# GpSimd's subtractions and scalings in pieces of 128 columns and of two token tiles

## The chip, the core and the metric

The kernel runs on one core of a Trainium2 chip. The core has five engines that work in parallel and each run their instructions in the order given: TensorE (PE, matrix products; its weight loads are shown as PEld), VectorE (DVE), ScalarE (ACT), GpSimd (POOL) and SyncE (SP, which here only issues DMAs). They wait for each other through semaphores. The metric is the time of one execution on the device, in microseconds (us); lower is better.

## The reference

Four batches of 10048 tokens with 128 channels go through agent attention (49 agents) and then through a mixture of 16 experts in 4 groups:

```
a2k = softmax(scale * agents @ k.T);  agent_v = a2k @ v
q2a = softmax(scale * q @ agents.T);  x = q2a @ agent_v
g = argmax(x @ w_group);  e = argmax(x @ w_expert[g])        # one expert per token
out = g_w * e_w * (relu(x @ w1[g, e]) @ w2[g, e])            # g_w, e_w: softmax weights
```

All inputs and the output are float32.

## The kernel before

A batch is cut into 79 token tiles of 128 tokens, and the loads into chunks of 8 tiles (1024 columns of the transposed k or q). Float32 values are split into two float16 numbers, a high and a low part, so that TensorE can multiply them at float16 speed. For a chunk of k or q: SP loads `xf`; ACT copies it to float16 (`xh`); POOL subtracts, `xl = xf - xh` (function `low`, in pieces of `PIECE` columns); TensorE then computes the scores of the 8 tiles against the agents, three products a tile (`xh` with the agents' high and low part, `xl` with the high part). The product with `xl` waits for the piece of `xl` that holds its tile.

For queries, DVE subtracts the maximum, ACT takes the exponential (`ef`) and copies it to float16 into `rows`, POOL subtracts again (the low part, columns NA to 2 NA of `rows`; `query_split`), TensorE transposes `rows` (`et`), and computes the router's logits from it. For keys, DVE takes running maxima (`mch`), ACT the exponential, and TensorE the agent values.

Routing, the counts of tokens per expert and the choice of the batch's most frequent expert are long chains of small DVE operations (`routing`, `output_weight`, `peaks` with its tile `pm`, `signed_weights` with the tiles whose names begin with f, p and m, `cntf` and `hot`). They end in weights for the batch (`wbuf`).

The main stream (`first`, `second`, `check`) multiplies each group of four tiles with those weights: products `ph`, ACT and DVE make `hh` and `hl` from them, products `po`, and the check `pv`. `rows_out` brings the result into SBUF: for batches after the first ACT copies it (`oo`) and POOL multiplies it by the token's weight `cw`, two tiles at a time; otherwise DVE does both at once. SP stores it.

The order of the work on every engine is fixed by the string `PLAN`: each letter takes the next step of one stream (m the main stream, a agents, q queries, w routing and weights, s stores, g gathers), and all engines are pinned to that order. Before it, `front` lays out the first batch by the list `ORDER`. Both stay as they are.

Of the kernel before, what the change touches and what calls it, by code (L numbers as in the profile page):

```python
# [22 lines left out]
P = 128  # L23
B = 4
N = 10048
C = 128
# [69 lines left out]
FEW = 3 * CT  # L96
ETS = 28
LAG = 3
PIECE = 2 * P
BUSY = [3, 12]  # L100


# [93 lines left out]
def build(ctx, tc, qT, kT, v, agT, wr, w1, w2, cpk, out):  # L196
    nc = tc.nc
    pe, vec, act, pool, sync = [Pinned(x) for x in (nc.tensor, nc.vector, nc.scalar, nc.gpsimd, nc.sync)]
# [83 lines left out]
    state = {}  # L282
# [30 lines left out]
    def split_steps(kind, b, ci):  # L313
# [10 lines left out]
        yield FINE  # L324
        low(pool, PIECE, xf, xh, xl, n // 2)
        yield FINE
        low(pool, PIECE, xf, xh, xl, n, n // 2)
        return xh, xl

    def low(eng, step, xf, xh, xl, n, first=0):  # L330
        for i in range(first, n, step):
            y = slice(i, min(i + step, n))
            eng.tensor_sub(out=xl[:, y], in0=xf[:, y], in1=xh[:, y])
# [145 lines left out]
    def front(b, early, order, later):  # L479
# [34 lines left out]
        for x in order:  # L514
# [16 lines left out]
            elif o in "lL":  # L531
                xf, m = hold[c]
                xh, xl = hold["x", f"h{c}" if o == "l" else "q"]
                if o == "l" and c in POOLED:
                    low(pool, PIECE, xf, xh, xl, m)
                else:
# [57 lines left out]
            elif o == "G":  # L594
                vec.tensor_copy(out=se, in_=small[0:NA, P + NA:P + NA + 1])
            elif o == "r":
                all_of(query_split(b, 0, query, True))
            elif o == "t":
                all_of(query_turn(b, 0, query, True))
# [89 lines left out]
    def queries_of(b, early=None, cs=None, *more):  # L689

        cs = list(range(len(chunks))) if cs is None else cs
        xs = [{} for _ in chunks]
        stages = [query_load, query_scores, query_exp, query_split, query_turn]
        groups = [[lambda b, ci, x, early: load_only("q", b, ci)]] + [stages[:1], stages[1:2], stages[2:4], stages[4:]]

        def run(group):
            def f(i):
                for stage in group:
                    yield from stage(b, cs[i], xs[cs[i]], early)
            return f  # L700

        yield from skewed(len(cs), *[run(g) for g in groups], *[lambda i, f=f: f(b, cs[i]) for f in more])
# [26 lines left out]
    def query_split(b, ci, x, early):  # L729
        t0, t1 = chunks[ci]  # L730
        ef = x["ef"][:, 0:t1 - t0]
        if early and ci % 2 == 0:
            pool.tensor_copy(out=rows[:, t0:t1, 0:NA], in_=ef)
        else:
            act.activation(rows[:, t0:t1, 0:NA], ef, AF.Copy)
        yield FINE
        whole = early or b == 0 and ci <= FIRST
        for i in range(0, t1 - t0, t1 - t0 if whole else 3):
            y = slice(i, t1 - t0 if whole else min(i + 3, t1 - t0))
            w = slice(t0 + y.start, t0 + y.stop)  # L740
            (vec if whole else pool).tensor_sub(out=rows[:, w, NA:2 * NA], in0=ef[:, y], in1=rows[:, w, 0:NA])
        yield
# [579 lines left out]
    def natural(b, w):  # L1322

        t, n = TILES[w]
        return dict(b=b, w=w, t=t, n=n, per=1, units=FULL, et=state[b]["et", w], apart=b > 0 and (b < LB or w < NW - 2),
                    wb=wbuf[b % 2].bitcast(F16), done=rows_out, **signed(w, 1, MODES))
# [4 lines left out]
    def rows_out(x):  # L1331

        po, b, n, t = x["po"], x["b"], x["n"], x["t"]
        o = mo.tile([P, TQ, C], F32, name="oo", bufs=4)
        if x["apart"]:
            act.activation(o[:, 0:n], po[:, 0:n], AF.Copy)
            yield
            for i in range(0, n, 2):
                y = slice(i, min(i + 2, n))
                pool.tensor_mul(out=o[:, y], in0=o[:, y], in1=state[b]["cw"][:, t + y.start:t + y.stop].broadcast_to([P, y.stop - y.start, C]))  # L1340
                if y.stop == n:
                    written.append((b, n, t, o))
                yield
        else:
            vec.tensor_mul(out=o[:, 0:n], in0=po[:, 0:n], in1=state[b]["cw"][:, t:t + n].broadcast_to([P, n, C]))
            written.append((b, n, t, o))
            yield
# [510 lines left out]
```

## Time and profile before

| | |
|---|---|
| median of 3 runs | 803.74 us (799.58 to 804.38) |
| the profiled execution | 802.54 us, span 800.7 us |
| busy share of the span | PE 84%, DVE 80%, ACT 63%, POOL 47% |
| POOL: subtractions for xl | 284 operations, 196 us |
| POOL: scalings of oo | 116 operations, 73.8 us |
| POOL: subtractions for rows | 108 operations, 43.6 us |

The span runs from the first to the last instruction in the trace. A row of the profile groups operations of one engine with the tiles that they write and read; "128x256 f16<-128x256 f32" is 128 partitions by 256 columns, output and input. Nearly all operations have the line of one helper (L180), so they are told apart by their tiles. The granted clock of TensorE is given as a share of 2.4 GHz; a stretch with a value between 0.5 and 1 mixes both levels. In the chain of waits, each piece is the work that the next one had to wait for. The number after x is the count of operations that a row merges.

### The profile page before, as it was taken

The numbers are of one execution on the slowest core, as the hardware profiler recorded it, in microseconds if no ns is written. First come the engines' busy times: TensorE is split into PE (matmuls) and PEld (weight loads), VectorE is DVE, ScalarE is ACT, GpSimd is POOL, SyncE is SP. The second block draws the span as 40 slices with busy tenths as digits, with TensorE's granted clock in tenths as the row PEclk, the third lists the DMA queues.
The fourth block names the chain that finished last, engine by engine and source line by source line (L and its number), as shares of the span: only waits on it lengthen the run. The fifth ranks groups of instructions, "written<-read, shape, count | busy, mean of one in ns | idle before, by whom it ended". The sixth has DMA issues, their size and how long they took to land.

```text
span 800.7 us, 22170 instructions
## 1 busy us (share of the span) xinstructions
PE 671.0 (84%) x8835; PEld 535.4 (67%) x8835; DVE 641.5 (80%) x1449; ACT 501.1 (63%) x1087; POOL 378.7 (47%) x619
## 2 busy tenths in 40 slices
PE   7864879989956799999766847789999989999994
PEld 6653758767844587788545736676788667877773
DVE  6869978967789785777998897968978998866663
ACT  4544479779934446899455323545968787467772
POOL 4126393139922433587365316852565233842220
PEclk9975889999977699999878965999999999999997
DMA  8845043695607518352285032155422444211211
GB/s 320 326 159 169 28 148 106 181 359 150 193 18 258 182 31 292 96 156 79 83 299 171 1 105 69 30 152 170 123 72 83 126 174 125 71 52 54 68 54 54
DMA packets 66273, 107.87 MB, mean 135 GB/s; under 512 B 5223, under 2 KB 46136, under 8 KB 65776
## 3 DMA queue, kind: packets, MB, share of 16 engines
q1 hardware_dynamic: 64816, 104.54, 40.3%
q0 software_dynamic: 1344, 1.82, 1.0%
q8 instruction: 71, 1.16, 0.6%
q14 instruction: 42, 0.34, 0.1%
HBM read 73.97 MB, written 32.47 MB: 133 GB/s over the span
## 4 chain that ended last, share of the span: by engine, by line
PE 43%; DVE 23%; issue 6%; ACT 4%; DMA 4%; POOL 4%; SPq 0%; POOLq 0%; ACTq 0%; DVEq 0%
PE at L180 16%; PE po L180 15%; PE ph L180 8%; PE pv L180 4%; DVE hl L180 2%; DVE pm L180 2%; DVE hot L180 2%; POOL xl L180 2%; DMA vf<-v 1%; DMA out<-oo 1%; POOL oo L180 1%; DMA xf<-qT 1%; DVE rd L180 1%; DVE oh L180 1%; DVE mch L180 1%
## 5 line engine op out<-in xcount | busy, mean ns | idle before, releaser
L180 POOL TENSOR_TENSOR xl<-xf,xh 128x256 f16<-128x256 f32 (+2 forms) x280 | 193.4, 722 | 158.7 <-ACT xh L180 149.2
L180 DVE SCALAR_TENSOR_TENSOR hl<-ph,hh 128x512 f16<-128x512 f32 (+1 forms) x256 | 172.2, 678 | 77.4 <-ACT hh L180 76.2
L180 PE MATMUL po<-wbuf,hh 128*128 128x128 f16 x1896 | 194.4, 225 | 0.0
L180 PEld LDWEIGHTS <-hh 128*128 128x128 f16 x2022 | 166.3, 101 | 34.4 <-issue 4.7
L180 PE MATMUL po<-wbuf,hl 128*128 128x128 f16 x948 | 178.8, 225 | 2.6 <-DVE hl L180 2.6
L180 ACT ACTIVATE hh<-ph 128x512 f16<-128x512 f32 (+1 forms) x256 | 152.0, 594 | 32.5 <-PE ph L180 28.0
L180 PE MATMUL ph<-et,wbuf 98*128 98x512 f16 x480 | 148.8, 393 | 5.2 <-ACT spare L180 4.6
L180 ACT ACTIVATE spare<-pv 128x512 bf16<-128x512 f32 (+1 forms) x164 | 97.4, 594 | 80.3 <-PE pv L180 70.0
L180 POOL TENSOR_TENSOR oo<-oo,cw 128x256 f32<-128x256 f32 x116 | 73.8, 656 | 130.8 <-ACT oo L180 120.4
L180 PEld LDWEIGHTS <-hl 128*128 128x128 f16 x1011 | 101.7, 101 | 3.1 <-DVE hl L180 3.1
L180 PE MATMUL pv<-et,wbuf 98*128 98x512 f16 x240 | 95.1, 396 | 0.1
L180 ACT ACTIVATE xh<-xf 128x1024 f16<-128x1024 f32 (+2 forms) x78 | 81.2, 1045 | 12.5 <-DMA xf<-kT 7.8
L180 PEld LDWEIGHTS <-wbuf 98*128 98x128 f16 x720 | 61.4, 102 | 35.6 <-issue 13.8
L180 PEld LDWEIGHTS <-et 98*128 98x128 f16 x1264 | 66.2, 100 | 22.6 <-issue 4.9
L180 PE MATMUL at<-agh,xl 128*128 128x49 f16 (+1 forms) x545 | 60.9, 192 | 19.1 <-POOL xl L180 18.9
L180 PEld LDWEIGHTS <-xh 128*128 128x128 f16 (+1 forms) x1264 | 64.8, 101 | 17.2 <-ACT xh L180 7.1
L180 PEld LDWEIGHTS <-xl 128*128 128x128 f16 (+1 forms) x632 | 54.3, 99 | 25.9 <-POOL xl L180 24.3
L180 POOL TENSOR_TENSOR rows<-ef,rows 128x147 f16<-128x147 f32 (+1 forms) x108 | 43.6, 432 | 57.7 <-ACT rows L180 46.0
L180 PE MATMUL at<-agh,xh 128*128 128x49 f16 (+1 forms) x545 | 61.6, 191 | 6.7 <-ACT xh L180 6.1
L180 DVE TENSOR_REDUCE flags<-pv 128x1 f32<-128x512 f32 (+1 forms) x92 | 62.2, 677 | 5.0 <-PE pv L180 4.9
L180 PE MATMUL at<-agl,xh 128*128 128x49 f16 (+1 forms) x545 | 61.1, 191 | 0.0
L180 PE MATMUL at<-vf,S 128*49 128x129 f32 (+1 forms) x632 | 45.5, 282 | 8.8 <-ACT S L180 5.8
(369 smaller groups left out, 1275.4 us busy)
## 6 DMA issues: line engine op xcount, KB each, us to landing
xf<-qT SPq DMA_DIRECT2D x38, 512.0 KB, 5.3
out<-oo SPq DMA_DIRECT2D x76, 256.0 KB, 4.0
vf<-v SPq DMA_DIRECT2D x36, 516.0 KB, 5.1
xf<-kT SPq DMA_DIRECT2D x35, 512.0 KB, 4.8
erow<-rows SPq DMA_DIRECT2D x3, 1975.0 KB, 7.5
wsl<-wkept SPq DMA_DIRECT2D x6, 544.0 KB, 4.2
w2f<-w SPq DMA_DIRECT2D x6, 512.0 KB, 4.5
w1f<-w SPq DMA_DIRECT2D x5, 512.0 KB, 4.9
```

The source lines that it names most:

```text
L180: y = f(*a, **k)
```

## The change

`PIECE` goes from 256 to 128 columns, so a chunk of 1024 columns is subtracted in eight operations and not in four. In `query_split` the pieces of `rows` hold two tiles and not three: a chunk of eight tiles has four pieces (2, 2, 2, 2) and had three (3, 3, 2). In `rows_out` each tile of `oo` is scaled by an operation of its own; the steps of the generator are the same two tiles, so `PLAN` meets the same number of steps.

```diff
-PIECE = 2 * P
+PIECE = P
...
         whole = early or b == 0 and ci <= FIRST
-        for i in range(0, t1 - t0, t1 - t0 if whole else 3):
-            y = slice(i, t1 - t0 if whole else min(i + 3, t1 - t0))
+        for i in range(0, t1 - t0, t1 - t0 if whole else 2):
+            y = slice(i, t1 - t0 if whole else min(i + 2, t1 - t0))
             w = slice(t0 + y.start, t0 + y.stop)
             (vec if whole else pool).tensor_sub(out=rows[:, w, NA:2 * NA], in0=ef[:, y], in1=rows[:, w, 0:NA])
...
             for i in range(0, n, 2):
-                y = slice(i, min(i + 2, n))
-                pool.tensor_mul(out=o[:, y], in0=o[:, y], in1=state[b]["cw"][:, t + y.start:t + y.stop].broadcast_to([P, y.stop - y.start, C]))
-                if y.stop == n:
+                for y in range(i, min(i + 2, n)):
+                    pool.tensor_mul(out=o[:, y], in0=o[:, y], in1=state[b]["cw"][:, t + y].broadcast_to([P, C]))
+                if y + 1 == n:
                     written.append((b, n, t, o))
```

POOL's order late in the second batch's queries (about 200 to 217 us of the trace), before; `xl` is the low part of a chunk, `rows` the float16 pair of the queries' exponentials, the last column the shape and the count:

```order
L180 TENSOR_TENSOR xl<-xf,xh 128x256 x6
L180 TENSOR_TENSOR rows<-ef,rows 128x3x49 x2
L180 TENSOR_TENSOR rows<-ef,rows 128x2x49
L180 TENSOR_TENSOR xl<-xf,xh 128x256 x3
L180 TENSOR_TENSOR xl<-xf,xh 128x192
L180 TENSOR_TENSOR xl<-xf,xh 128x256
L180 TENSOR_TENSOR xl<-xf,xh 128x192
```

The same place after the change:

```order
L180 TENSOR_TENSOR xl<-xf,xh 128x128 x12
L180 TENSOR_TENSOR rows<-ef,rows 128x2x49 x4
L180 TENSOR_TENSOR xl<-xf,xh 128x128 x7
L180 TENSOR_TENSOR xl<-xf,xh 128x64
L180 TENSOR_TENSOR xl<-xf,xh 128x128 x3
L180 TENSOR_TENSOR xl<-xf,xh 128x64
```

Nothing has moved: each operation stands where its larger one stood, in two parts. The half chunk of 448 columns becomes three pieces of 128 and one of 64.

TensorE at the scores of a chunk, where the product with `xl` waits for POOL (the rest of TensorE's order is the same):

```order
 L180 LDWEIGHTS xh
 L180 MATMUL ph<-agl,xh 128x49
-L180 LDWEIGHTS xl
+L180 LDWEIGHTS xl [waits Pool_49]
 L180 MATMUL ph<-agh,xl 128x49
 L180 LDWEIGHTS xh
```

The second tile of each pair now has a wait of its own, where it had stood behind that of the first. DVE, ACT and SP have the same instructions in the same order.

## Rows read from the trace of the kernel before

**Rows 1.** The page's part 1: busy time, share, instructions.

```profile
PE 671.0 (84%) x8835; PEld 535.4 (67%) x8835; DVE 641.5 (80%) x1449; ACT 501.1 (63%) x1087; POOL 378.7 (47%) x619
```

**Rows 2.** Stages: length, busy us of PE, PEld, DVE, ACT, POOL, then clock, DMA.

```profile
60.00:118.00 58.00, 39.22 (x503) 32.74 (x502) 52.20 (x129) 32.86 (x63) 38.26 (x61) 0.72 0.38 119
170.00:218.00 48.00, 44.69 (x831) 36.30 (x832) 36.09 (x73) 44.27 (x89) 44.51 (x82) 1.00 0.69 211
340.00:382.00 42.00, 42.00 (x716) 34.19 (x714) 32.02 (x54) 39.22 (x81) 34.34 (x64) 1.00 0.40 115
382.00:425.00 43.00, 30.57 (x328) 21.94 (x326) 38.85 (x72) 23.18 (x51) 22.67 (x27) 0.80 0.53 180
```

**Rows 3.** Chain of waits, 168 to 218 us: start, us, what.

```profile
197.20 2.56 POOL xl L180 x4
199.79 0.94 POOL rows L180 x3
200.93 2.57 POOL xl L180 x4
```

**Rows 4.** POOL's instructions in time: start, us, what; the second merges two shapes.

```profile
183.36 5.08 POOL L180 TENSOR_TENSOR xl<-xf,xh 128x256 f16<-128x256 f32 x8
...
367.30 2.33 POOL L180 TENSOR_TENSOR xl<-xf,xh 128x256 f16<-128x256 f32 x4
```

**Rows 5.** POOL's groups by shape: busy us, mean ns, idle us before and its releasers.

```profile
L180 POOL TENSOR_TENSOR xl<-xf,xh 128x256 f16<-128x256 f32 x266 | 186.3, 731 | 158.7 <-ACT xh L180 149.2 <-PE at L180 9.3
L180 POOL TENSOR_TENSOR oo<-oo,cw 128x256 f32<-128x256 f32 x114 | 73.0, 661 | 130.8 <-ACT oo L180 120.4 <-issue 10.4
L180 POOL TENSOR_TENSOR rows<-ef,rows 128x147 f16<-128x147 f32 x72 | 32.4, 471 | 57.7 <-ACT rows L180 46.0 <-PE ph L180 10.0 <-PE at L180 1.6
L180 POOL TENSOR_TENSOR rows<-ef,rows 128x98 f16<-128x98 f32 x32 | 11.6, 363 | 0.0
...
L180 POOL TENSOR_TENSOR oo<-oo,cw 128x128 f32<-128x128 f32 x2 | 0.8, 395 | 0.0
```

**Rows 6.** POOL alone by stage, for xl, then rows, then oo.

```profile
170.00:218.00 48.00, 34.05 (x54) 1.00 0.69 211
...
340.00:382.00 42.00, 17.73 (x28) 1.00 0.40 115
...
170.00:218.00 48.00, 10.68 (x27) 1.00 0.69 211
...
340.00:382.00 42.00, 7.60 (x20) 1.00 0.40 115
...
340.00:382.00 42.00, 9.55 (x16) 1.00 0.40 115
```

**Rows 7.** DVE in time: two operations beside POOL's xl, two without POOL.

```profile
66.52 0.59 DVE L180 SCALAR_TENSOR_TENSOR fva<-fqq,fmu 128x8 f32<-128x8 f32 x1
67.14 0.60 DVE L180 TENSOR_SCALAR fva<-fva 128x8 f32<-128x8 f32 x1
...
279.39 0.17 DVE L180 TENSOR_TENSOR pinc<-ways 128x16 f32<-128x16 f32 x1
279.60 0.17 DVE L180 TENSOR_TENSOR pinc<-pinc,pun 128x16 f32<-128x16 f32 x1
```

**Rows 8.** DVE in time: hot without POOL, and beside it.

```profile
280.21 0.88 DVE L180 TENSOR_SCALAR hot<-wide,ppos 128x512 f16<-128x512 f16 x3
...
439.45 4.49 DVE L180 TENSOR_SCALAR hot<-wide,ppos 128x512 f16<-128x512 f16 x8
```

**Rows 9.** Waits of PE: whole span, 60 to 118 us, 382 to 425 us: us, times, longest.

```profile
PE at L180 <- POOL xl L180: 18.9, 43, 1.2
...
PE at L180 <- DVE cntf L180: 6.3, 1, 6.3
...
PE at L180 <- POOL xl L180: 9.3, 14, 1.2
```

**Rows 10.** POOL in time, from 405.4 us: eight pieces beside DVE's pm.

```profile
406.12 9.70 POOL L180 TENSOR_TENSOR xl<-xf,xh 128x256 f16<-128x256 f32 x8 [2.28 <-ACT xh L180]
```

## The prediction

> **What bounds the kernel now.** I read the page's busy shares first. TensorE (PE) is busy for 84% of the span, VectorE (DVE) for 80%, ScalarE (ACT) for 63% and GpSimd (POOL) for 47% [rows 1], so no engine is the bound throughout, and an average says nothing about POOL. The table by stage says it: from 170 to 218 us POOL is busy for 44.51 of 48.00 us, beside ACT at 44.27 and PE at 44.69; from 340 to 382 us POOL has 34.34 of 42.00 and PE is full; from 60 to 118 and from 382 to 425 us DVE is the fullest (52.20 of 58.00, 38.85 of 43.00), POOL has room, and the granted TensorE clock is 0.72 and 0.80 of full speed, a mix of the two levels 1.2 and 2.4 GHz [rows 2]. So two kinds of stage have to be kept apart: in the first POOL paces, in the second DVE's chain of small operations paces and POOL only disturbs it. The chain of waits confirms the first: from 197.2 to 203.5 us it runs through POOL alone, four subtractions of xl, three of rows, four of xl [rows 3].
>
> **The change, part by part.** The order is unchanged on every engine; operations are split in place. DMAs and queues are the same. TensorE waits for xl once per 128 columns in place of once per 256, and I cost those waits at nothing, since they only matter where the piece is late.
>
> *Price of a split.* Four xl pieces of 256 columns take 2.56 us [rows 3], eight 5.08, and four pieces of 256, 192, 256 and 192 take 2.33 [rows 4]. So a 256 piece costs (5.08 - 2.56) / 4 = 0.63 from start to start, 128 columns are worth 2.56 - 2.33 = 0.23, and a piece of 128 comes to 0.40: two of them 0.80, 0.17 us more than before. The scalings show both sizes: 661 ns for 256 columns and 395 for 128, so a split adds 2 x 395 - 661 = 129 ns [rows 5]. I take 0.15 us for a split xl or oo (bounds 0.13 and 0.17). Rows pieces: 471 + 471 + 363 = 1305 ns become 4 x 363 = 1452, 0.15 us for a group of three by these means [rows 5], of which some 0.03 per added piece is overhang into the next: 0.11. Over the kernel that is about 280 xl and 114 oo splits (59 us) and 36 groups of rows (4 us): some 63 us more POOL work. How much of it lies on the path is a matter of stages.
>
> The same rows, read by duration alone, would be cheaper. The Trainium skill, Perfetto Trace Analysis, section "GPSIMD Engine Instruction", says that POOL spans are unreliable and that start-to-start spacing should be used. By spans, 731 ns for 256 columns [rows 5] (which holds waits) against 2 x 395 would price a split at only 0.06 us: +2 in place of +6.5 at 170 us, 0 and +1 for the next two terms, and the sum below would end near 799; by spacing it ends at 806.
>
> *170 to 218 us.* 54 xl pieces and 27 rows pieces, nine groups, run there [rows 6]: 54 x 0.15 + 9 x 0.11 = 9.1 us. POOL then needs 44.5 + 9.1 = 53.6 us in a stage of 48.0. If all its present gaps are filled the stage grows by 5.6; if they stay, by 9.1. I take **+6.5**, since ACT, the engine that releases POOL, gets idle time and runs ahead. The stage ends in the last queries, on which DVE's routing waits, so it passes through. The lower bound is +4, if pieces that arrive earlier let PE start earlier.
>
> *340 to 382 us.* 28 xl, 20 rows (about seven groups) and 16 oo [rows 6] add 4.2 + 0.8 + 2.4 = 7.4 us to 34.34, so 41.7 of 42.00: the idle time just covers it, and whatever is not where the idle time is comes out. I take **+1** (bounds 0 and +4).
>
> *Chunks that PE waits for elsewhere.* PE waits 43 times for xl, 18.9 us in all, 9.3 of them from 382 to 425 [rows 9]. Some ten chunks outside 170 to 218 have PE waiting for their last piece; each comes 0.6 us later, 6 us, and about half hides behind DVE's chain: **+3**. A place that I watch: at 406 us eight pieces take 9.70 us [rows 10] in place of 5.08 [rows 4], because DVE's long operations on pm go in between; with sixteen pieces more of them can.
>
> *What DVE gets back.* A DVE operation on SBUF operands that comes while POOL works is held up: small ones that follow each other every 0.21 us alone follow every 0.62 beside POOL [rows 7], and 0.63 is just the spacing of POOL's pieces: one DVE operation gets in per piece. Eight hot operations take 4.49 us beside POOL at 439 us, where three alone take 0.88 [rows 8], so 8 would take some 2.2. By each form's shortest against its others, of which these are two, I count about 130 held operations and 45 us, some 32 of them in the DVE-paced stages (60 to 118, 218 to 300, 382 to 530). With pieces of 0.40 a hold shrinks from 0.41 to about 0.18, but there are twice as many pieces to meet. If holds double, 260 x 0.18 = 47 us: no gain. If they stay, 130 x 0.23 = 30 us: the other bound. Where a run of 13 held operations meets 12 pieces, as from 60.5 to 68 us, some 20 would be held: 13 x 0.41 = 5.3 against 20 x 0.18 = 3.6, a third less. A third of 32 is 11; about 70% of that lies on the chain, PE waiting behind it (6.3 us for cntf alone [rows 9]): **-8** (0 to -16).
>
> The Trainium skill, SBUF — State Buffer, section "Who interferes with whom", says that a GpSimd operation and a DVE one with two SBUF inputs exclude each other for the whole instruction. By that, what DVE can lose grows with POOL's whole time, 280 x 0.63 = 176 us to 560 x 0.40 = 224, by 27%, and the third saved turns into some 9 us lost, 6 of them on the chain: 820 in place of 806. The row shows a hold of 0.41 where a piece takes 0.63, so in this trace DVE gets in during the rest.
>
> *Everything else.* From 700 us on, PE sets the pace and POOL's scalings have room. +0.5 for the stages not named.
>
> **Sum:** +6.5 + 1 + 3 + 0.5 - 8 = +3.0 us on the profiled execution's 802.54 us, which stands 1.2 us under the median of 803.74. So 805.5 to 806.7: **806 us**, no change that could be told apart from none, since about 1% (8 us) is what a measurement of this kernel can tell.
>
> **Rivals.**
> *POOL paces two stages and DVE gets nothing (slower).* The place is 170 to 218 us. If ACT's waits for POOL keep POOL's own gaps in place, this stage gives the full +9, the one at 340 +4, the late chunks +4, and DVE's holds double in number: 802.5 + 17 = 819.5; with a third of DVE's gain, 815. It decides once POOL's gaps in 170 to 218 do not shrink below some 2 us. For it: POOL and ACT are both above 92% there. Against: ACT would have less to do per us. Chance 0.25.
> *PE's clock falls (slower).* In 170 to 218 PE is 93% busy and the clock is 1.00; in the stages where PE is busy for 71% and less (382 to 425: 30.57 of 43.00) it is 0.80 [rows 2]. At +6.5 PE would be busy for 82%. If a 7 us piece of it went to 1.2 GHz, its matmuls would take twice as long: some +3, hence 809, or 822 on top of the rival above. I give 0.04 of the slower chance to it. The Trainium skill, TensorE: Matmul & The Clock Gate, Part 1, says that an idle array is throttled; whether many waits of 0.6 us count as idle no row here shows.
> *POOL's hold grows with its work (slower).* If the 0.41 is not a fixed part less than the piece but the piece's whole time as DVE meets it, holds of 0.40 at twice the number leave DVE 6 us later on its chain in place of 8 earlier: 820. The small operations near 66 us speak against it, spaced by one piece and no more [rows 7]; 0.03 of the slower chance. The lock rule above is this case.
> *DVE's relief wins (faster).* If holds stay at 130 and shrink, -16 on the chain, and POOL's gaps take up part of the rest: +4 + 0 + 2 - 16 = -10, about 793. For it: the gaps of PE before cntf are long and the chain in them is DVE's. Against: pieces double, and POOL would have to be seldom alone. Chance 0.13.
> *The split is not dearer.* If the fixed price per operation is hidden by the next one, 128 columns would take 0.32 and POOL's work would not grow: -8 or so, 795. The 192-column row speaks against it: 0.02 of the 0.13.
>
> **How the numbers follow.** The forecast (within 1%, 795.7 to 811.8) has 0.60, its own range being 799 to 811; slower than that 0.26, faster 0.14. The range to 80% reaches into the slower rival to 815 and into the faster to 796.
>
> **What would show it.** In the profile after: xl pieces spaced at 0.39 to 0.40 us (price right); POOL over 95% busy from 170 on and that stage 54 to 55 us long (first term); the small DVE operations near 66 us spaced at some 0.4 us, and the gap of PE before cntf below 5 us (DVE term); PE's waits for xl up from 18.9 to some 25 us. The prediction is wrong if the stage at 170 does not grow, or if DVE's small operations are held as often as there are pieces.

## The result, and the profile after

The changed kernel takes 812.71 us (median of 4 runs, 808.34 to 815.0) where the kernel before takes 804.06: ratio 1.0104, 95% interval 1.0068 to 1.014. A second set of runs (12 of the change, 35 of the kernel before, which takes 812.03 us there) gave 1.0045 (1.0009 to 1.0081). Ratios and intervals leave out executions in a slow state, and they are not quotients of the medians. So the change costs about 0.5 to 1%: 3.6 to 8.4 us, where +3 was forecast. The forecast was 806 us and no change that could be told apart from none; a small loss can be told, in both sets. The range of 796 to 815 held the time.

The profiled execution of the changed kernel took 808.34 us, 5.8 more than that of before. It is the fastest of the four, 4.4 us under their median, so the trace accounts for some 6 of the 8.4 us. The page's part 1, then the table by stage (length, busy us of PE, PEld, DVE, ACT, POOL, then clock, DMA share, GB/s):

```profile
PE 690.7 (86%) x8835; PEld 543.4 (67%) x8835; DVE 627.9 (78%) x1449; ACT 503.3 (62%) x1087; POOL 451.6 (56%) x1053
```

```profile
60.00:118.00 58.00, 42.17 (x489) 33.13 (x490) 51.53 (x132) 34.46 (x64) 44.14 (x107) 0.71 0.39 119
170.00:218.00 48.00, 44.19 (x718) 34.29 (x719) 30.58 (x64) 40.26 (x78) 43.83 (x118) 0.96 0.68 223
...
340.00:382.00 42.00, 41.55 (x696) 33.10 (x694) 31.49 (x53) 38.10 (x75) 42.00 (x117) 1.00 0.40 115
382.00:425.00 43.00, 31.97 (x369) 22.84 (x367) 37.63 (x72) 25.06 (x57) 28.30 (x60) 0.83 0.49 171
```

Against [rows 1]: POOL has 72.9 us more work, DVE 13.6 less with the same 1449 operations; those are the two sides of the change. Against [rows 2]: from 340 to 382 us POOL is busy for all of the 42.00 us (before 34.34). From 170 to 218 us its share has not risen, because the stage now begins later (first piece at 172.75, before at 170.16); at 218 us it is not over. POOL in time shows the stage whole; these are its first and last rows, and between them the two chunks that answer to the first of [rows 4]:

```profile
172.75 3.46 POOL L180 TENSOR_TENSOR xl<-xf,xh 128x128 f16<-128x128 f32 x8 [26.31 <-ACT xh L180]
...
186.58 6.22 POOL L180 TENSOR_TENSOR xl<-xf,xh 128x128 f16<-128x128 f32 x16
...
202.87 3.12 POOL L180 TENSOR_TENSOR xl<-xf,xh 128x128 f16<-128x128 f32 x8
205.96 1.33 POOL L180 TENSOR_TENSOR rows<-ef,rows 128x98 f16<-128x98 f32 x4
...
229.41 1.24 POOL L180 TENSOR_TENSOR rows<-ef,rows 128x98 f16<-128x98 f32 x4
```

From 172.75 to 230.65 it is 57.9 us. In the kernel before the same stretch runs between these two rows, 50.6 us:

```profile
170.16 2.88 POOL L180 TENSOR_TENSOR xl<-xf,xh 128x256 f16<-128x256 f32 x4 [27.51 <-ACT xh L180]
...
219.68 1.10 POOL L180 TENSOR_TENSOR rows<-ef,rows 128x147 f16<-128x147 f32 x3
```

The other side is DVE. The operations of [rows 7] in the changed kernel, beside POOL again:

```profile
67.62 0.35 DVE L180 SCALAR_TENSOR_TENSOR fva<-fqq,fmu 128x8 f32<-128x8 f32 x1
68.01 0.35 DVE L180 TENSOR_SCALAR fva<-fva 128x8 f32<-128x8 f32 x1
```

They follow each other every 0.39 us, where it was 0.62. PE's waits over the whole span, as in [rows 9]:

```profile
PE at L180 <- POOL xl L180: 14.5, 28, 1.1
PE at L180 <- DVE cntf L180: 10.5, 4, 4.4
```

and from 60 to 118 us:

```profile
PE at L180 <- DVE cntf L180: 3.7, 1, 3.7
```

The wait for `cntf` there has gone from 6.3 to 3.7 us.

**Where the time went.** ACT runs the same instructions in the same order in all kernels here, so the start of one and the same ACT instruction in two traces says how far one lies behind the other. The table has, for stretches of the kernel before, how much each kernel lost (+) or gained (-) in it (medians of five neighbouring instructions; "again" is the change in the second set, the other names are the experiments below):

```
stretch (us)  change  again  xl only  oo only  rows only  not at 170  h5    h4    h1    h3 (64)
  0- 45        +3.1   +2.0    +0.8     +0.4      +0.1       +0.5     +0.5  +0.7  +1.2   +1.7
 45- 99        -3.2   -2.1    -2.0     -0.4      -0.4       -3.0     -2.2  -3.5  -3.8   -0.4
 99-122        +3.1   +3.1    +2.8      0.0      +0.2       +3.1     +0.3  +0.1   0.0    0.0
169-224        +6.8   +9.1    +8.1     +0.2      +0.3       +0.8     +0.4   0.0   0.0    0.0
240-265        -2.6   -2.3    -1.7     -0.8       0.0       -1.7     -1.5  -0.1  -0.3   -0.1
265-272        +1.6   +1.0    +2.2      0.0       0.0       +2.3     +2.3  +0.8  +0.8   +3.3
272-283        -3.2   -2.8    -3.1     -0.8      -0.6       -3.1     -3.0  -3.0  -2.8   -0.9
320-385        +1.8   +1.9    +0.1     -0.1       0.0       +1.9     +1.9  -0.1   0.0    0.0
396-428        +4.2   +2.0    +4.5     -0.4      -1.7       +1.3     -1.5  -0.2  +2.7   +2.5
428-448        -3.3   -2.4    -2.4     -0.2       0.0       -2.3     -2.4  -1.4  -2.2   -3.3
506-640        -4.8   -4.6    -1.8     -4.2      -1.6       -5.2     -4.3  -3.8  +0.6   +3.7
```

Most entries agree from trace to trace within 1 us; 0 to 45, 396 to 428 and 506 to 640 do so less, and single entries there prove little. Each column is one execution, up to 6 us faster or 7 us slower than its kernel's median. The last stretch, from 640 us on, is left out: there "again", h5, h4, h1 and h3, all from other chips than the first four experiments, lose 7.9 to 12.2 us, whatever their edit, and the others at most 1.5.

For the change, the stretches shown lose 20.6 us and gain 17.1; those left out, none above 1.6, add 2.4, and it ends 5.9 us later. The entries at 265 to 272 and 272 to 283 belong together: what the first loses, the second gets back.

DVE too runs the same 1449 operations in the same order in all kernels of the table, so their durations can be subtracted one by one. In the changed kernel they are shorter by 3.4 us in all from 45 to 99, by 0.7 from 265 to 283, by 1.2 from 428 to 448 and by 6.7 from 506 to 640: there the gains are DVE's. From 240 to 265 us they are not shorter (+0.1). That gain is TensorE's clock: these 16 products, which stand in the kernel before in a piece of its chain of waits (the first row), take 3.65 us at a granted clock of 0.50 there (second row), and 1.99 at 1.00 in the changed kernel (third).

```profile
259.40 4.18 PE at L180 x18
```

```profile
259.92 3.65 PE L180 MATMUL at<-at,w1f 128*128 128x49 f32 x16
```

```profile
267.67 1.99 PE L180 MATMUL at<-at,w1f 128*128 128x49 f32 x16
```

They take 1.99 us in the five traces that gain 1.5 us or more in this stretch, and 3.65 in the others.

### The profile page after: what moved, and what is told of

Read it like the earlier page. It is cut to its first block, busy times and chain, and to the rows that moved or that the text cites. A ratio compares the mean times of both kernels' runs of the same rounds, so it can differ in the third digit from the quotient of the medians.

```text
span 806.5 us, 22606 instructions
## 1 busy us (share of the span) xinstructions
PE 690.7 (86%) x8835; PEld 543.4 (67%) x8835; DVE 627.9 (78%) x1449; ACT 503.3 (62%) x1087; POOL 451.6 (56%) x1053
## 4 chain that ended last, share of the span: by engine, by line
PE 37%; DVE 16%; POOL 4%; issue 3%; DMA 2%; ACT 2%; POOLq 0%; SPq 0%; DVEq 0%; ACTq 0%
PE po L180 14%; PE at L180 13%; PE ph L180 7%; PE pv L180 4%; DVE hl L180 3%; POOL xl L180 3%; DMA vf<-v 1%; DVE pm L180 1%; DVE hot L180 1%; DVE oh L180 1%; DVE pt L180 1%; DVE mtl L180 1%; DVE fqq L180 1%; DMA xf<-kT 1%; DMA er<-erow,gidx 1%
## 5 line engine op out<-in xcount | busy, mean ns | idle before, releaser
L180 POOL TENSOR_TENSOR xl<-xf,xh 128x128 f16<-128x128 f32 (+1 forms) x560 | 240.7, 467 | 123.8 <-ACT xh L180 123.1
L180 POOL TENSOR_TENSOR oo<-oo,cw 128x128 f32<-128x128 f32 x230 | 93.9, 440 | 116.5 <-ACT oo L180 105.1
L180 PE MATMUL at<-agh,xl 128*128 128x49 f16 (+1 forms) x545 | 70.0, 194 | 23.2 <-POOL xl L180 14.5
L180 PEld LDWEIGHTS <-xl 128*128 128x128 f16 (+1 forms) x632 | 56.4, 100 | 40.2 <-POOL xl L180 36.0
L180 PEld LDWEIGHTS <-xh 128*128 128x128 f16 (+1 forms) x1264 | 67.9, 102 | 16.1 <-ACT xh L180 6.2
L180 POOL TENSOR_TENSOR rows<-ef,rows 128x98 f16<-128x98 f32 (+1 forms) x144 | 49.3, 375 | 40.4 <-ACT rows L180 31.0
L180 PE MATMUL at<-agh,xh 128*128 128x49 f16 (+1 forms) x545 | 66.7, 192 | 5.4 <-ACT xh L180 5.4
L180 PE MATMUL at<-agl,xh 128*128 128x49 f16 (+1 forms) x545 | 66.1, 191 | 0.0
L180 PE MATMUL at<-vf,S 128*49 128x129 f32 (+1 forms) x632 | 47.5, 288 | 8.8 <-ACT S L180 5.3
```

What stands on the lines that cost most here:

```text
L180: y = f(*a, **k)
```

## The experiments

The ratios are to the kernel before on the same chip; it took 803.3 us beside the first four experiments, 812.0 beside the next four and 812.3 beside the last two. 1% is some 8 us. Where an expectation is given in us, it was meant for a chip on which the kernel before takes 804.

**Only the subtractions for xl.** The edit:

```diff
-PIECE = 2 * P
+PIECE = P
```

> Only PIECE goes to 128 columns; rows stay in pieces of three tiles, the scalings of oo at two. Theory A (the price of the split, paid where POOL paces, 170 to 218 us): xl carries 54 x 0.15 of the 9.1 us there, so nearly the whole loss is here, +5 to +8 us, 809 to 812, and the stage up to the routing after 218 us ends some 5.5 to 6 us later. Rival B (the scalings and rows, which hold buffers and feed TensorE's transposes, carry it): +1 to +3 us, 805 to 807.

Measured: 805.81 us, ratio 1.0056 (1.003 to 1.0082). The time lies in the rival's range, but the place is the first theory's: the loss of the change at 99 to 122 and 169 to 224 us is here in full, so it belongs to `xl` and not to `rows` or `oo`. The traced execution, 812.52 us, is the slowest of 12, and it loses even 8.1 at 169 to 224 with the rows as before. The traces point to a second effect, TensorE's clock. Two stretches of this kernel, columns as above:

```profile
172.00:182.00 10.00, 8.92 (x100) 6.87 (x101) 4.54 (x9) 5.92 (x13) 7.94 (x20) 0.66 0.92 331
182.00:190.00 8.00, 7.11 (x106) 5.29 (x102) 5.36 (x18) 6.71 (x14) 5.66 (x15) 1.00 0.31 86
```

From 172 to 182 us the granted clock is 0.66, so TensorE ran for about two thirds of that at 1.2 GHz; it was idle for 1.08 of those 10 us, nearly all of it before the clock fell at 174.5. Then ACT and POOL in time:

```profile
181.80 0.60 ACT L180 ACTIVATE spare<-pv 128x512 bf16<-128x512 f32 x1 [2.20 <-PE pv L180]
```

```profile
181.52 0.20 POOL L180 MEMSET av<- 32x129 f32 x1
184.34 3.13 POOL L180 TENSOR_TENSOR xl<-xf,xh 128x128 f16<-128x128 f32 x8 [2.62 <-ACT xh L180]
```

ACT waits 2.2 us for the slow TensorE, the copy `xh` stands behind that on ACT, and POOL, which paces, loses 2.62 us waiting for `xh`. The repeat of the change has the same dip (0.68) and the same hole before POOL's third chunk (2.27 us), and loses 9.1 there; the first trace of the change has a shorter one (below), and loses 6.8. In the nine traces with pieces of 256 or 512 columns in this stage the clock is 1.00 from 172 to 218 us. How often the dip comes is not known: "xl only" and the repeat were traced in executions 5 to 7 us above their medians.

**Only the scalings.** The edit:

```diff
-                y = slice(i, min(i + 2, n))
-                pool.tensor_mul(out=o[:, y], ...)
-                if y.stop == n:
+                for y in range(i, min(i + 2, n)):
+                    pool.tensor_mul(out=o[:, y], ...)
+                if y + 1 == n:
```

> Only the scalings of oo are split. Theory A: 114 splits of 0.13 to 0.15 us, POOL has room beside them but for 340 to 382 us (16 x 0.15 = 2.4 us): within 2 us of before, 803 to 806. Rival B: oo's buffers come free later and ACT and the stores follow: +4 us, 808.

Measured: 798.1 us, ratio 0.9941 (0.9911 to 0.9971), faster than either theory had it. The gain lies mostly at 506 to 640 us (-4.2), where POOL's scalings run beside DVE's chains. DVE's operations there are held less: the group `hot`, 493 to 545 us, in the kernel before and in this one (us, mean ns, idle before):

```profile
L180 DVE TENSOR_SCALAR hot<-wide,ppos 128x512 f16<-128x512 f16 x16 | 7.1, 513 | 1.5 <-PE at L180 1.5
```

```profile
L180 DVE TENSOR_SCALAR hot<-wide,ppos 128x512 f16<-128x512 f16 x16 | 5.0, 383 | 1.5 <-PE at L180 1.5
```

The 2.1 us of these sixteen are half of the stretch's gain. In the stage at 340 to 382 us these scalings alone cost nothing (-0.1), nor do the `xl` pieces alone (+0.1): both together do (+1.8 to +1.9, in four traces), since only both fill POOL. In the stretch that answers to 340 to 374 us of the kernel before, it is busy for 33.18 of 34.10 us with the `xl` pieces alone and all the time in the changed kernel (last of the busy times):

```profile
350.00:384.10 34.10, 34.10 (x600) 28.00 (x597) 26.60 (x45) 31.86 (x62) 33.18 (x82) 1.00 0.44 134
```

```profile
345.20:381.10 35.90, 35.45 (x599) 28.43 (x597) 26.91 (x46) 32.29 (x62) 35.90 (x100) 1.00 0.42 126
```

**Only the rows.** `query_split` takes two tiles for three, nothing else is changed.

> Only the pieces of rows go from three tiles to two. Theory A: nine groups of 0.11 us from 170 to 218 us, 1 us, and the same at 340 us hidden: 803 to 806. Rival B: TensorE's transposes wait for every piece: +3 us, 807.

Measured: 803.0 us, ratio 1.0003 (0.9973 to 1.0033), as the first theory had it. Ten more operations stand in the stage at 169 to 224 us, some 1.4 us of POOL's work; it lost 0.3.

The three parts do not add up to the whole: their ratios multiply to 1.000, and the change has 1.0045 to 1.0104. Two places are seen in the table, 340 to 385 us (together +1.8, apart +0.0) and 506 to 640 us (together -4.8, apart -7.6); the rest is not located.

**The whole change, but not in POOL's stage.** Pieces of 256 columns for the chunks between 170 and 224 us, and rows by three in that batch:

```diff
+    def piece(kind, b, ci):
+        return 2 * P if (kind, b) == ("q", 1) or kind == "k" and b == 2 and ci <= 2 else PIECE
...
+        step = piece(kind, b, ci)
-        low(pool, PIECE, xf, xh, xl, n // 2)
+        low(pool, step, xf, xh, xl, n // 2)
...
+        per = 3 if b == 1 else 2
```

> The whole change, but in the second batch's query stage (chunks q of batch 1, k of batch 2 up to 2; rows of batch 1) the pieces are those of before. Theory A: the 6 us that this stage lost come back: 805 to 808, some 6 us under the change. Rival C (the loss is spread over the waits of TensorE for xl elsewhere, or comes from a lower clock throughout): 810 to 813.

Measured: 797.24 us, ratio 0.9941 (0.991 to 0.9971). The same edits that cost 0.5 to 1% as a whole gain 0.6% with this one stage left out: it costs 0.8 us there in place of 6.8 to 9.1, and most other rows of the table stay. So this stage turns a gain into a loss. It comes out 8 us under the first theory's range of 805 to 808, which had only the 6 us of this stage coming back; the two ratios differ by 1.0 to 1.6%, 8 to 13 us, of which the table places 6 to 8 in the stage.

**The change again.** No edit.

> The change itself, timed again on the same chip as the next three. If the stage from 170 to 218 us costs the 6 to 7 us by which its end moved in the trace, and the rest of the change gains 6 (the run with the old pieces in that stage), this comes to 803 to 806. If something beyond the stage makes it dearer (the start, the clock), it stays at 811 to 814.

Measured: 817.65 us on a chip where the kernel before takes 812.03, ratio 1.0045 (1.0009 to 1.0081). The mean granted clock of its 12 executions is 0.899, that of the 35 of the kernel before 0.898: a lower clock throughout is not what makes the change slower. Where the kernel before takes 804 the ratio gives 807.6, between the two outcomes expected.

**Fine pieces only beside DVE's chains.** The kernel before, with 128 columns in 18 chunks (not the 23 of the expectation), in four stretches of its trace: 60 to 91, 263 to 274, 425 to 439 and 538 to 591 us.

```diff
+    def piece(kind, b, ci):
+        fine = {("q", 0): range(4, 7), ("k", 1): range(0, 4), ("k", 2): (7, 8), ("q", 2): (0,), ("k", 3): (7, 8), ("q", 3): (1, *range(3, 8))}
+        return P if ci in fine.get((kind, b), ()) else 2 * P
```

> The kernel before with xl in pieces of 128 only in 23 chunks that run beside DVE's chains (60 to 92, 266 to 276, 426 to 442 and 566 to 605 us); scalings and rows as before. Theory D (a hold of DVE lasts the piece less a fixed 0.2 us, so finer pieces shorten DVE's chains there and cost POOL time that it has): 797 to 800, 4 to 6 us under before. Rival E (DVE's gain came from the scalings alone): 802 to 804.

Measured: 808.12 us, ratio 0.9941 (0.991 to 0.9973), as theory D had it. It gains at 45 to 99, 272 to 283 and 428 to 448 us, as the change does, and loses nothing at 99 to 122 or at 169 to 224. Its fourth stretch brings nothing by the table (506 to 640: +0.6).

**Pieces of 512 columns in POOL's stage.** The kernel before with `4 * P` in the stage from 170 us on.

> The kernel before with pieces of 512 columns for xl in the stage from 170 to 218 us. Theory A (POOL paces there and pays a fixed price per operation): some 27 operations fewer, 27 x 0.15 = 4 us less POOL work; ACT and TensorE are at 92% there too, so the stage ends 1 to 3 us earlier: 800 to 802. Rival F (ACT paces the stage, and a first half that comes 0.5 us later costs): 803 to 806.

Measured: 812.11 us, ratio 0.9986 (0.9956 to 1.0016), the rival's outcome. POOL in time, two chunks of it:

```profile
184.32 2.27 POOL L180 TENSOR_TENSOR xl<-xf,xh 128x512 f16<-128x512 f32 x2
187.24 2.28 POOL L180 TENSOR_TENSOR xl<-xf,xh 128x512 f16<-128x512 f32 x2 [0.65 <-ACT xh L180]
189.53 1.19 POOL L180 TENSOR_TENSOR rows<-ef,rows 128x147 f16<-128x147 f32 x3
190.96 2.27 POOL L180 TENSOR_TENSOR xl<-xf,xh 128x512 f16<-128x512 f32 x2 [0.23 <-ACT xh L180]
```

A chunk is 0.29 us cheaper than with 256 columns, and what is saved comes back as waits for ACT's `xh`. From the first piece to the last rows the stage takes 51.0 us, where it was 50.6. So in the kernel before POOL and ACT pace this stage together: POOL less loaded gives nothing, POOL more loaded costs most of what it gets (the change gives POOL 9.2 us more to do there, 56.48 for 47.29, and the stage is 7.3 us longer).

**64 columns beside DVE's chains.** The kernel `h1`, with half its fine piece:

```diff
-        return P if ci in fine.get((kind, b), ()) else 2 * P
+        return P // 2 if ci in fine.get((kind, b), ()) else 2 * P
```

> As the run with 128 columns beside DVE's chains, but with 64 there. Theory D: a piece is spaced by 0.27 us, holds shrink to some 0.06 us or vanish, POOL needs 16 x 0.27 = 4.3 us a chunk in place of 3.1, and has it: DVE's holds in those chunks nearly gone, 1 to 3 us under the run with 128, 795 to 799, unless TensorE waits for the later last piece. Rival G (a hold is the whole piece and falls only in proportion, and there are more pieces to meet): no better than with 128, or 1 to 4 us worse for the later pieces.

Measured: 813.69 us, ratio 0.9999 (0.9966 to 1.0031): the gain is gone, as the rival had it. From 45 to 99 us DVE is not to blame; its operations there are 5.8 us shorter than in the kernel before (3.0 with 128 columns). The pair of [rows 7] in this kernel:

```profile
64.91 0.23 DVE L180 SCALAR_TENSOR_TENSOR fva<-fqq,fmu 128x8 f32<-128x8 f32 x1
65.17 0.23 DVE L180 TENSOR_SCALAR fva<-fva 128x8 f32<-128x8 f32 x1
```

now follows every 0.26 us. But sixteen pieces of a chunk take this long on POOL:

```profile
277.46 4.25 POOL L180 TENSOR_TENSOR xl<-xf,xh 128x64 f16<-128x64 f32 x16 [1.28 <-ACT xh L180]
```

and TensorE's waits from 60 to 118 us are, for 128 columns and for 64:

```profile
PE at L180 <- POOL xl L180: 5.7, 18, 0.5
PE at L180 <- DVE cntf L180: 3.7, 1, 3.7
```

```profile
PE at L180 <- POOL xl L180: 12.3, 37, 1.2
...
PE at L180 <- DVE cntf L180: 1.7, 1, 1.7
```

What `cntf` gives (3.7 to 1.7 us), `xl` takes (5.7 to 12.3): there the bound moves from DVE to POOL.

Later it is DVE that loses. Its operations from 506 to 640 us are 1.8 us longer than in the kernel before (with 128 columns 2.3 shorter), because of two that were held not for one piece but through a train of POOL's operations. One of them, 0.16 us long in all other kernels here, and what POOL did meanwhile:

```profile
582.37 3.32 DVE L180 TENSOR_TENSOR ppos<-ppos,ways 128x8 f32<-128x8 f32 x1
```

```profile
582.14 1.19 POOL L180 TENSOR_TENSOR oo<-oo,cw 128x256 f32<-128x256 f32 x2
583.29 1.19 POOL L180 TENSOR_TENSOR rows<-ef,rows 128x147 f16<-128x147 f32 x3
584.43 0.62 POOL L180 TENSOR_TENSOR oo<-oo,cw 128x256 f32<-128x256 f32 x1
585.00 1.13 POOL L180 TENSOR_TENSOR xl<-xf,xh 128x64 f16<-128x64 f32 x4
```

The other takes 2.73 us; earlier there are a `fkey` at 274.35 us with 1.67 and an `mtv` at 89.40 with 1.44. The change has such a hold too, for 0.52 us in the kernel before:

```profile
110.85 4.48 DVE L180 TENSOR_TENSOR oh<-lg 128x240 f16<-128x240 f32 x1
```

It is in the three traces with fine `xl` and `rows` there (4.4 to 4.5 us); "xl only" lacks it and loses as much at 99 to 122 us, so it does not make that loss. Why these few were not let in between two pieces stays open.

**Both gains together.** `h1` and the scalings by one tile; the rows as before.

> The kernel before, with the two edits that each ran at 0.994 of it: lower-half pieces of 128 columns only in the chunks beside VectorE's chains (three groups, around 60-85, 265-275 and 425-440 us), and GpSimd's scalings of the outputs by one token tile at a time; all other pieces and the subtractions for the rows stay as before. Theory A (VectorE is given back its holds in different places by the two edits, so the gains add): 0.985 to 0.991 of the kernel before, 792 to 797 us where before runs at 804. Rival B (the two gains are one: what is given back early is slack that the later chains use up): 0.993 to 0.996, as each alone, 798 to 801 us.

Measured: 801.44 us where the kernel before takes 812.29, ratio 0.9858 (0.9824 to 0.9892). The product of the two ratios is 0.988, so they add. This is the lowest ratio here; the interval of the next experiment overlaps it.

**Coarse wherever TensorE waits.** The kernel of the fourth experiment (not at 170), with pieces of 256 columns also in the chunks of 99 to 122 and 385 to 415 us:

```diff
+        coarse = {("q", 1): range(99), ("k", 2): range(3), ("k", 1): range(4, 99), ("q", 0): range(7, 99), ("k", 3): range(3, 6)}
-        return 2 * P if (kind, b) == ("q", 1) or kind == "k" and b == 2 and ci <= 2 else PIECE
+        return 2 * P if ci in coarse.get((kind, b), ()) else PIECE
```

> The whole change, but with pieces of 256 columns and rows by three in GpSimd's stage (170-224 us), and pieces of 256 columns also in the other chunks whose lower half TensorE waits for at once (the last of the first batch, 99-122 us, and three of the last batch, 385-415 us). Theory A (such a chunk costs its 0.56 us directly, there is no second cover): the +3 us that the trace of the kernel with only GpSimd's stage undone shows at 99-122 goes, and of its later +1 to +2 us at 396-428 a part: 0.988 to 0.991 of the kernel before, 794 to 797 us where before runs at 804. Rival B (those delays are made up by the next wait anyway): 0.993 to 0.996, as with only GpSimd's stage undone.

Measured: 801.5 us against 812.29, ratio 0.9878 (0.984 to 0.9916). The 3.1 us at 99 to 122 are 0.3 now, as the first theory said; the intervals of this and of the fourth experiment overlap by a hair, so the 0.6% between the two is likely; the table places half of it, 2.8 us, at 99 to 122.

## Why the prediction was right or wrong

**The price of a split: right.** Forecast 0.15 us, eight pieces in 3.2; measured 3.12 a chunk where it was 2.56, so (3.12 - 2.56) / 4 = 0.14. With 512 and 64 columns, 2.27 and 4.25 us a chunk, each piece more costs 0.145 and 0.14: one fixed price over an eightfold range of sizes. Rows: four in the place of three end 0.14 us later (1.33 for 1.19), 0.11 was forecast. The groups by shape (busy us, mean ns) answer to [rows 5]:

```profile
L180 POOL TENSOR_TENSOR xl<-xf,xh 128x128 f16<-128x128 f32 x546 | 236.4, 469 | 123.8 <-ACT xh L180 123.1 <-PE at L180 0.4
L180 POOL TENSOR_TENSOR oo<-oo,cw 128x128 f32<-128x128 f32 x230 | 93.9, 440 | 116.5 <-ACT oo L180 105.1 <-issue 10.6 <-PE ph L180 0.8
L180 POOL TENSOR_TENSOR rows<-ef,rows 128x98 f16<-128x98 f32 x140 | 48.4, 378 | 40.4 <-ACT rows L180 31.0 <-PE ph L180 9.5
```

The step in which a rule of the Trainium skill was weighed (Perfetto Trace Analysis, "GPSIMD Engine Instruction": trust the spacing, not the span) came out for the rule: a mean span of 469 ns stands beside a spacing of 390.

**170 to 218 us, +6.5: right in size, the reason only half.** It lost 6.8 in the first trace, 9.1 in the second. The prediction had POOL pacing this stage before. The experiment with 512 columns showed that ACT paces as much as POOL; the step held because the change only adds work. What was left out is the clock: it was a rival with 0.04, and a small form of it happened, in all three traces with split pieces here. In the first trace of the change it is this stretch:

```profile
195.00:200.00 5.00, 5.00 (x83) 4.48 (x81) 3.05 (x6) 3.73 (x9) 5.00 (x15) 0.66 0.49 161
```

There POOL is busy throughout, so the slow TensorE cost little; where it came earlier, it left POOL without `xh` for 2.3 to 2.6 us, about what those two traces lose beyond the first. Why it falls then and not before stays open: in the kernel before TensorE is busy for only 2.48 of 4.00 us from 168 to 172, and no fall follows. Short falls stand at other places too, far from any edit: in the trace with 512 columns the clock is 0.50 from 319.4 to 322.6 us.

**340 to 382 us, +1: measured +1.8**, within its bounds of 0 and +4, and only with both kinds of split.

**Chunks that TensorE waits for, +3: 3.1 shown, at one place and uncovered.** 99 to 122 us alone lost 3.1, which taking those chunks coarse undid: little of it hid behind DVE's chain. The 1.6 at 265 to 272 comes back right after. The 4.2 at 396 to 428 (2.0 in the repeat) cannot be laid to the change: the two kernels with fine pieces only beside DVE's chains have the old pieces from 385 to 420 us and lose 2.7 and 2.5 there. The list of signs was wrong here: TensorE's waits for `xl` were to rise from 18.9 to 25 us and fell to 14.5. The total of such rows is no measure of the delay. From 105.70 to 107.62 us the changed kernel's products with `xl` follow each other every 0.38 us, at POOL's spacing, and hardly any of these short waits stands in PE's row (0.3 us from 99 to 125). At 406 us the answer to [rows 10] is sixteen pieces in 10.53 us, so that place lost little.

**What DVE gets back, -8: the mechanism right, the size too small.** Counting what lies more than 0.08 us above each form's shortest duration in the kernel before, held operations went from 128 to 166, their mean from 0.347 to 0.199 us, the sum from 44.4 to 33.1. (With the shortest of both traces it is 144 to 169, and 49.1 to 33.7.) The holds shrank to about what was forecast (0.18), and rose by 30% or less, where 50% was taken. On the path it gave some 13 us by the table (45 to 99, 265 to 283, 428 to 448 and 506 to 640), and DVE's own operations there are 12.0 us shorter, within the bounds of 0 to 16. Two figures of the prediction's working were off: of the 13 operations that it counted as held from 60.5 to 68 us nine were, by 3.2 us and not 5.3; and 815 in its first rival, "with a third of DVE's gain", should have been 817. What was missed is the scalings. They were costed as POOL's work and as nothing for DVE, and alone they gave 0.6%; from 506 to 640 us they make DVE's operations 4.3 us shorter, the smaller pieces of `rows` alone 3.1.

The rival that holds grow with POOL's work falls: with 256, 128 and 64 columns POOL's pieces follow every 0.63, 0.39 and 0.27 us, and DVE's small operations every 0.62, 0.39 and 0.26. As a rule DVE gets in once per piece; the few that were held through a train, above, are the exception, and neither the prediction nor its rivals had them. In these traces the rule of the Trainium skill (SBUF — State Buffer, "Who interferes with whom") therefore does not cost DVE the time by which POOL's work grew, as 820 us would have asked.

**The sum: near, in part by luck.** The losses shown to be the change's are 6.8, 1.8 and 3.1, together 11.7 where 11.0 was forecast. DVE gave some 4 to 5 us more than the 8 forecast, and TensorE's clock another 1.7 that no term had. By that the change should have been faster. What made up for it in the first trace, 3.1 us in the first 45 ("xl only", with the same pieces there, shows 0.8) and 4.2 at 396 to 428, no run lays to the change. (In the repeat the same terms come to +1.5.) So +3.0 forecast and +5.9 in the trace are near each other not because every term held.

## What to carry to other kernels

Where one engine's train of operations holds up another's, the size of a piece is not one number for a kernel: small pieces let the other engine in, and cost a fixed 0.14 us each where the engine paces or someone waits for the last piece. Set it by stage: the edit made everywhere cost 0.5 to 1.0%, while fine subtractions only beside DVE's chains, with the scalings by one tile, gained 1.4%. And hold gains and losses against the trace apart, stretch by stretch, and against the durations of the engine that is to gain: a sum that comes out near can hide terms that are off, and a gain can be the clock's.

## What the runs showed that was not expected

- GpSimd's subtraction on 128 partitions costs 0.14 us per instruction beside its columns, from 64 to 512 columns alike (2.27, 2.56, 3.12 and 4.25 us for 1024 columns).
- A small DVE operation that meets a train of such pieces mostly takes the spacing of one piece (0.62, 0.39, 0.26 us), down from 0.62 to nearly its own 0.21 with 64 columns. A few are held through many pieces: 4.4 to 4.5 us in three traces, 1.4 to 3.3 us four times in the kernel with 64 columns.
- A stage that is 7 us longer for TensorE's suppliers had the granted clock at 0.66 to 0.68 for 5 to 10 us, with TensorE busy for 80 to 100% of it, in three traces of three; with the old pieces it was 1.00 there.
